# Scaling the gradient before its transposes, and placing filler steps by a PE budget, in a fused attention and FFN backward kernel

## The chip, the cores and the metric

The kernel runs on one core of a Trainium2 chip. The metric is the device time of one execution in microseconds (us). Every time below is the median of several runs, and a span is the length of the one profiled run. The granted TensorE clock and the span are listed for each run. A run that is more than 1.5% above the fastest of its kernel counts as slow and is left out of ratios.

The engines go by the names of the profile: PE (TensorE) does the matmuls, DVE (VectorE) and POOL (GpSimd) element-wise work, ACT (ScalarE) exponentials and copies, and SP (SyncE) issues DMAs, as ACT and POOL also do here. SBUF is the working memory on the chip; PE writes its results to PSUM, in banks. An "extra" is a DVE operation other than the product Pd that runs between two products. A "ring" is a circle of steps in which each waits for the one before.

## The reference

The forward function mixes windowed attention and a gated FFN with a sigmoid gate. The kernel returns the output and the gradients of seven inputs, so eight tensors.

```python
# S = 2048, D = 512, H = 32 heads of 16, window 256, F = 1376, bf16
g = sigmoid((x * gate_w).sum(-1, keepdims=True))
qkv = x @ wqkv                                  # A: attention
p = softmax(where(band_of_256, q @ k.T * 16**-0.5, -1e9))
a = (p @ v) @ wo
gate, up = x @ W_gate, x @ W_up                 # B: FFN
b = (gate * (gate > 0) * up) @ W_down
out = g * a + (1 - g) * b
out, vjp = jax.vjp(forward, x, wqkv, wo, W_gate, W_up, W_down, gate_w)
return out, *vjp(grad_out)
```

## The kernel before

The kernel has four stages. A **start** transposes `x` and `grad_out` and computes the first of four projections. An **attention loop** of 384 slots follows. A slot computes scores S and score gradients dP for one unit, the exponential Pt of S on ACT, a mask on POOL and the product Pd of Pt and dP on DVE. Sums over Pt and Pd feed small per-stage tasks. FFN and further projection work fills PE between them. A **transition** loads and transposes weights and the attention results. Then come the **dw pass** (weight gradients) and the **output pass** (output and dx).

```python
# one slot: PE writes S and dP, ACT makes Pt, POOL masks it, DVE makes Pd
u.S  = ps.tile([P, 2, W], F32, tag="S",  bufs=1)       # two PSUM banks
u.dP = ps.tile([P, 2, W], F32, tag="dP", bufs=1)       # two PSUM banks, one buffer
nc.scalar.activation(u.Pt[:, :, :u.width], u.S[:, :, :u.width], ACT.Exp)
nc.gpsimd.affine_select(...)                            # mask, in place on Pt
nc.vector.tensor_tensor(out=u.Pd[...], in0=u.Pt[...], in1=u.dP[...], op=ALU.mult)

# the FFN step that the change makes lighter on DVE
dhs = fp.tile([P, W], BF, tag="dhs", bufs=1)
nc.vector.scalar_tensor_tensor(out=dhs[:fs, :], in0=g_bc[:fs, sl], scalar=1.0, in1=dhps[:fs, :],
                               op0=ALU.subtract, op1=ALU.mult, reverse0=True)

# what fills PE in each slot: one projection step if one is open, then FFN by even share
def fill(frac):
    if projs:
        try: next(projs[0])
        except StopIteration: projs.pop(0)
    while dense["done"] < frac * TOTAL:
        dense["done"] += next(ffn)        # front of a chunk in turn with the back of the one before
# ... (cut)

# transition: SP loads dqT, dkvT, OT; ACT's queue loads the weights
for c in range(DC):
    nc.sync.dma_start(dqT[:, c, :], dqo_v[0, c])
# ... dkvT, OT (cut)
nc.scalar.dma_start(Wg_sb6[:], ...)
nc.scalar.dma_start(Wu_sb6[:], ...)
nc.scalar.dma_start(wqkv_sb6[:], ...)
nc.scalar.dma_start(Wd_sb[:, :nfull, :], ...)
nc.scalar.dma_start(Wd_sb[:fsz(nfull), nfull, :], ...)   # the last part of Wd
nc.scalar.dma_start(wo_sb6[:], ...)
# then PE transposes Wg, Wu, wqkv; ACT and DVE copy the results in turn
```

Of the kernel before, what the change touches and what calls it, by code (L numbers as in the profile page):

```python
# [46 lines left out]
def kernel(  # L47
# [64 lines left out]
    with ExitStack() as win:  # L112
# [23 lines left out]
        big = win.enter_context(tc.tile_pool(name="big", bufs=1))  # L136
        x_T = big.tile([P, DC, S], BF, name="x_T")
        go_T = big.tile([P, DC, S], BF, name="go_T")
        db_r = big.tile([P, NT, D], BF, name="db_r")
        g_bc = big.tile([P, S], F32, name="g_bc")  # L140

        ps = win.enter_context(tc.tile_pool(name="ps", bufs=1, space=PSUM))
        wp = win.enter_context(tc.tile_pool(name="wp", bufs=2))
        fp = win.enter_context(tc.tile_pool(name="fp", bufs=2))
        ap_ = win.enter_context(tc.tile_pool(name="ap", bufs=2))
# [45 lines left out]

        flip = {"i": 0}
# [8 lines left out]
        def rows_to_T(dst, src, sb):  # L201
            for cp in range(2):
                pt = tr_bank(8)
                for c in range(2):
                    for k in range(4):
                        nc.tensor.transpose(pt[:, 4 * c + k, :], src[:, 4 * sb + k, (2 * cp + c) * P:(2 * cp + c + 1) * P],
                                            ident[:])
                evac2(dst[:, 2 * cp:2 * cp + 2, sb * W:(sb + 1) * W].rearrange("p c s -> p c s"),
                      pt.rearrange("p (c k) s -> p c (k s)", c=2))

        def proj(c, evac):
            w3, wo_r = wsets.pop(("p", c))
            pt = tr_bank(4)
            for jc in range(DC):
                nc.tensor.transpose(pt[:, jc, :], wo_r[:, jc * P:(jc + 1) * P], ident[:])
            woT = wp.tile([P, DC, P], BF, tag="woT")
            evac(woT[:], pt)
            yield 0.3
            for sb in range(NSB):
                sl = slice(sb * W, (sb + 1) * W)  # L220
                for which in (1, 2, 0, 3):
                    pp = mm_bank()
                    for cd in range(DC):
                        if which < 3:
                            nc.tensor.matmul(pp[:], lhsT=w3[:, cd, which, :], rhs=x_T[:, cd, sl],  # L225
                                             start=(cd == 0), stop=(cd == DC - 1))
                        else:
                            nc.tensor.matmul(pp[:], lhsT=woT[:, cd, :], rhs=go_T[:, cd, sl],
                                             start=(cd == 0), stop=(cd == DC - 1))
                    cs = wp.tile([P, W], BF, tag="cs", bufs=2)  # L230
                    if which == 0:
                        nc.scalar.mul(cs[:], pp[:], scale)
                    elif which < 3:
                        evac(cs[:], pp[:])
                    else:
                        nc.vector.tensor_tensor(out=cs[:], in0=pp[:], in1=g_bc[:, sl], op=ALU.mult)  # L236
                    dst_d, w = ((QD_d, 0), (KV_d, 0), (KV_d, 1), (QD_d, 1))[which]
                    nc.sync.dma_start(dst_d[c][sb].rearrange("(h w d) s -> w h d s", w=2, d=Dh)[w], cs[:])
                    yield 0.87

        def ffn_front(fc):
            fs, f0 = fsz(fc), fc * P
            wg, wu, wd = wsets.pop(("f", fc))
            if fc + 1 < FC:
                load_ffn(fc + 1)
            pt = tr_bank(4)
            for c in range(DC):
                nc.tensor.transpose(pt[:, c, :fs], wd[:fs, c * P:(c + 1) * P], ident[:fs, :fs])
            wdT = wp.tile([P, DC, P], BF, tag="wdT")
            nc.scalar.copy(wdT[:, :, :fs], pt[:, :, :fs])  # L250
            yield 0.3
            rows = []
            for tg in range(NSB):
                sl = slice(tg * W, (tg + 1) * W)
                hT = fp.tile([P, W], BF, tag="hT")
                dgT = fp.tile([P, W], BF, tag="dgT")
                duT = fp.tile([P, W], BF, tag="duT")
                gps = mm_bank()
                for c in range(DC):
                    nc.tensor.matmul(gps[:fs, :], lhsT=wg[:, c, :fs], rhs=x_T[:, c, sl],  # L260
                                     start=(c == 0), stop=(c == DC - 1))
                rg = fp.tile([P, W], BF, tag="rg")
                nc.scalar.activation(rg[:fs, :], gps[:fs, :], ACT.Relu)
                yield 0.87
                ups = mm_bank()
                for c in range(DC):
                    nc.tensor.matmul(ups[:fs, :], lhsT=wu[:, c, :fs], rhs=x_T[:, c, sl],
                                     start=(c == 0), stop=(c == DC - 1))
                upm = fp.tile([P, W], BF, tag="upm")
                nc.vector.scalar_tensor_tensor(out=upm[:fs, :], in0=rg[:fs, :], scalar=0.0,  # L270
                                               in1=ups[:fs, :], op0=ALU.is_gt, op1=ALU.mult)
                nc.gpsimd.tensor_tensor(out=hT[:fs, :], in0=rg[:fs, :], in1=upm[:fs, :], op=ALU.mult)  # L272
                yield 0.87
                dhps = mm_bank()
                for c in range(DC):
                    nc.tensor.matmul(dhps[:fs, :], lhsT=wdT[:, c, :fs], rhs=go_T[:, c, sl],
                                     start=(c == 0), stop=(c == DC - 1))
                dhs = fp.tile([P, W], BF, tag="dhs", bufs=1)
                nc.vector.scalar_tensor_tensor(out=dhs[:fs, :], in0=g_bc[:fs, sl], scalar=1.0, in1=dhps[:fs, :],  # L279
                                               op0=ALU.subtract, op1=ALU.mult, reverse0=True)  # L280
                nc.vector.tensor_tensor(out=dgT[:fs, :], in0=dhs[:fs, :], in1=upm[:fs, :], op=ALU.mult)
                nc.gpsimd.tensor_tensor(out=duT[:fs, :], in0=dhs[:fs, :], in1=rg[:fs, :], op=ALU.mult)  # L282
                for w, src_t in enumerate((hT, dgT, duT)):
                    nc.sync.dma_start(ffn_d[fc, w, :fs, sl], src_t[:fs, :])
                rw = fp.tile([P, 4, 3, P], BF, tag="rows", bufs=6)
                if fs == P:
                    nc.sync.dma_start_transpose(out=rw[:].rearrange("p k w f -> p k (w f)"),
                                                in_=ffn_d[fc, :, :, sl].rearrange("w p s -> (w p) s"))
                else:
                    for w in range(3):  # L290
                        nc.sync.dma_start_transpose(out=rw[:, :, w, :fs], in_=ffn_d[fc, w, :fs, sl])
                rows.append(rw)
                yield 0.87
            wsets["r", fc] = rows

        def ffn_back(fc):
            fs, f0 = fsz(fc), fc * P
            rows = wsets.pop(("r", fc))
            wst = fp.tile([P, DC, 2, P], BF, tag="wst", bufs=1)
            for c in range(DC):  # L300
                wps = mm_bank()
                for t in range(NT):
                    nc.tensor.matmul(wps[:, 0:2 * fs], lhsT=x_r[:, t, c * P:(c + 1) * P],  # L303
                                     rhs=rows[t // 4][:, t % 4, 1:3, :fs], start=(t == 0), stop=(t == NT - 1))
                    if t == NT // 2 - 1:
                        yield 0.9
                nc.scalar.copy(wst[:, c, :, :fs], wps[:, 0:2 * fs].rearrange("p (a f) -> p a f", a=2))
                yield 0.9
            nc.sync.dma_start(out_4[:, f0:f0 + fs].rearrange("(c p) f -> p c f", p=P), wst[:, :, 0, :fs])
            nc.sync.dma_start(out_5[:, f0:f0 + fs].rearrange("(c p) f -> p c f", p=P), wst[:, :, 1, :fs])  # L310
            dps = mm_bank()
            for t in range(NT):
                nc.tensor.matmul(dps[:fs, :D], lhsT=rows[t // 4][:, t % 4, 0, :fs], rhs=db_r[:, t, :],  # L313
                                 start=(t == 0), stop=(t == NT - 1))
                if t % 4 == 3 and t < NT - 1:
                    yield 0.87
            dst = fp.tile([P, D], BF, tag="dst", bufs=1)
            nc.scalar.copy(dst[:fs, :], dps[:fs, :D])
            nc.sync.dma_start(out_6[f0:f0 + fs, :], dst[:fs, :])
            yield 0.87  # L320
# [520 lines left out]
```

## Time and profile before

| | before |
|---|---|
| median of the first 4 runs | 1201.27 us (1195.23 to 1206.71) |
| profiled span | 1193.5 us |
| first Pd starts | 51.1 us |
| last Pd ends | 840.3 us |
| first dw matmul | 908.8 us |
| first matmul of the output pass | 1003.4 us |

These moments are read from the instruction timeline. The stages therefore last 51, 789, 68.5, 95 and 190 us.

First, four lines of the profile page of the kernel before. Line one is the span. The second gives busy time, share of the span and number of instructions per engine. The other two cut the span into 40 slices of 30 us: busy tenths of PE, and the granted PE clock in tenths.

```profile
span 1193.5 us, 25074 instructions
...
PE 1002.2 (84%) x9607; PEld 469.9 (39%) x9748; DVE 707.7 (59%) x876; ACT 562.6 (47%) x751; POOL 633.8 (53%) x1019
...
PE   5688789999888888888889999889128886999997
...
PEclk9889999999999999999999999999657999999999
...
```

PE is busy nearly all the time except in the slices after the loop, where its clock falls too. That is the transition.

The table of stretches of the kernel before gives, for each stretch, its length, then busy time and (in brackets) instruction count per engine, then the granted clock, the DMA share and GB/s.

```profile
...
core 0: us, PE busy (x) PEld busy (x) DVE busy (x) ACT busy (x) POOL busy (x), PEclk, DMA share, GB/s
100.00:700.00 600.00, 531.65 (x6214) 242.83 (x6308) 476.65 (x516) 383.23 (x490) 438.83 (x725) 0.99 0.49 123
845.00:905.00 60.00, 15.43 (x120) 12.80 (x121) 7.17 (x18) 8.70 (x15) 7.80 (x11) 0.50 0.79 257
...
```

In 600 us of the loop PE is busy 89% and DVE 79%. In the transition PE has half its clock and is busy 26%. The Trainium skill, page "TensorE: Matmul & The Clock Gate", section "What's actually happening", says that PE falls to half rate after an idle window of about 3.4 us. The trace agrees on the half rate: the clock is 0.50 here and 0.99 in the loop. How long an idle stretch it takes is not read from this table.

The longest of PE's waits in the loop of the kernel before, 130 to 775 us (who waits for whom, total us, number, longest):

```profile
...
PE dP L424 <- DVE Pd L462: 32.4, 87, 1.0
...
```

Two lines of the groups of the same loop, shapes kept apart: busy us and mean ns of one, then idle time of the engine just before them and what ended it.

```profile
...
L462 DVE TENSOR_TENSOR Pd<-Pt,dP 128x1024 bf16<-128x1024 bf16 x242 | 294.7, 1218 | 84.4 <-PE dP L424 39.8 <-PE S L424 23.6 <-ACT Pt L457 7.1
...
L279 DVE SCALAR_TENSOR_TENSOR dhs<-g_bc,mm 128x512 bf16<-128x512 f32 x33 | 22.5, 683 | 1.9 <-PE mm L276 1.5
...
```

The product takes 1.22 us, and the step to be removed from DVE takes 0.68.

The instruction timeline of the transition of the kernel before (start, duration, engine and line, operation; in brackets the idle time before and what ended it; ACTq and SPq are DMA issues):

```profile
...
847.86 0.46 ACTq L668 DMA_DIRECT2D Wg_sb<-in_B_W_gate_dram  x1
848.37 0.52 ACTq L669 DMA_DIRECT2D Wu_sb<-in_B_W_up_dram  x1
...
868.90 0.38 ACTq L670 DMA_DIRECT2D wqkv_sb<-in_A_wqkv_dram  x1
...
876.80 0.37 ACTq L671 DMA_DIRECT2D Wd_sb<-in_B_W_down_dram  x1
877.21 8.34 ACTq L673 DMA_DIRECT2D Wd_sb<-in_B_W_down_dram  x1
887.01 0.49 ACTq L674 DMA_DIRECT2D wo_sb<-in_A_wo_dram  x1
...
887.55 1.07 ACT L650 COPY WgT_sb<-pt 128x512 bf16<-128x512 bf16 x2 [45.75 <-DMA Wd_sb<-in_B_W_down_dram]
888.18 2.12 PE L679 MATMUL pt<-ident,Wg_sb 128*128 128x128 bf16 x14 [16.95 <-ACT WgT_sb L650]
...
```

ACT's DMA issues run from 847.86 to 887.01, and ACT's first copy waits behind them. PE could go on with the weight transposes only at 888.18.

### The profile page before, as it was taken

The numbers are of one execution on the slowest core, as the hardware profiler recorded it, in microseconds if no ns is written. First come the engines' busy times: TensorE is split into PE (matmuls) and PEld (weight loads), VectorE is DVE, ScalarE is ACT, GpSimd is POOL, SyncE is SP. The second block draws the span as 40 slices with busy tenths as digits, with TensorE's granted clock in tenths as the row PEclk, the third lists the DMA queues.
The fourth block names the chain that finished last, engine by engine and source line by source line (L and its number), as shares of the span: only waits on it lengthen the run. The fifth ranks groups of instructions, "written<-read, shape, count | busy, mean of one in ns | idle before, by whom it ended". The sixth has DMA issues, their size and how long they took to land. (4 is left out here: it accounts for less than half of the span.)

```text
span 1193.5 us, 25074 instructions
## 1 busy us (share of the span) xinstructions
PE 1002.2 (84%) x9607; PEld 469.9 (39%) x9748; DVE 707.7 (59%) x876; ACT 562.6 (47%) x751; POOL 633.8 (53%) x1019
## 2 busy tenths in 40 slices
PE   5688789999888888888889999889128886999997
PEld 4233434434343443433444343444025442444443
DVE  2247787867788866788788888787102122222322
ACT  5345667666666655666666666665013221111010
POOL 2736787856777855778777778675110001221221
PEclk9889999999999999999999999999657999999999
DMA  7257554454643544445553544322780014545330
GB/s 203 77 136 187 124 128 122 112 143 109 132 120 104 134 124 119 121 107 123 122 129 103 127 103 123 85 74 63 197 308 34 19 45 135 175 130 159 102 107 23
DMA packets 267242, 142.81 MB, mean 120 GB/s; under 512 B 161201, under 2 KB 261970, under 8 KB 267122
## 3 DMA queue, kind: packets, MB, share of 16 engines
q1 hardware_dynamic: 236514, 115.08, 37.2%
q10 hardware_dynamic: 28224, 19.70, 5.4%
q0 software_dynamic: 2384, 6.43, 1.7%
q8 instruction: 76, 1.25, 0.5%
q14 instruction: 44, 0.36, 0.1%
HBM read 59.05 MB, written 52.59 MB: 94 GB/s over the span
## 5 line engine op out<-in xcount | busy, mean ns | idle before, releaser
L462 DVE TENSOR_TENSOR Pd<-Pt,dP 128x1024 bf16<-128x1024 bf16 (+2 forms) x384 | 442.0, 1151 | 145.2 <-PE dP L424 76.0
L457 ACT ACTIVATE Pt<-S 128x1024 bf16<-128x1024 f32 (+2 forms) x384 | 372.6, 970 | 203.1 <-PE S L424 174.0
L434 POOL TENSOR_SCALAR_AFFINE_SELECT Pt<-Pt 128x256 bf16<-128x256 bf16 (+1 forms) x736 | 348.3, 497 | 165.3 <-ACT Pt L457 158.0
L303 PE MATMUL mm<-rw,x_r 128*128 128x256 bf16 (+1 forms) x704 | 101.7, 272 | 5.9 <-DMA rw<-ffn_d 5.8
L424 PEld LDWEIGHTS <-kv 32*128 32x128 bf16 x1408 | 54.3, 92 | 116.9 <-issue 109.3
L424 PE MATMUL dP<-dO,kv 32*128 32x128 bf16 (+2 forms) x704 | 74.5, 275 | 25.8 <-DVE Pd L462 22.4
L424 PE MATMUL dP<-kv,dO 32*128 32x384 bf16 (+2 forms) x704 | 73.0, 273 | 17.0 <-DVE Pd L462 14.5
L771 ACT COPY a_sb<-aps 128x512 f32<-128x512 f32 x16 | 9.4, 586 | 160.9 <-issue 78.6
L424 PE MATMUL S<-Q,kv 32*128 32x128 bf16 (+2 forms) x704 | 79.3, 276 | 4.6 <-ACT Pt L457 3.5
L424 PE MATMUL S<-kv,Q 32*128 32x384 bf16 (+2 forms) x704 | 76.9, 275 | 2.6 <-ACT Pt L457 1.9
L303 PEld LDWEIGHTS <-x_r 128*128 128x128 bf16 x704 | 59.3, 98 | 40.9 <-issue 28.5
L705 POOL DMA_DIRECT2D go_t<-in_grad_out_dram x16 | 8.7, 543 | 121.1 <-DVE da_t L707 105.9
L797 PE MATMUL dxps<-WgT_sb,dgT_g 128*128 128x512 bf16 (+1 forms) x176 | 66.7, 379 | 0.8
L272 POOL TENSOR_TENSOR hT<-rg,upm 128x512 bf16<-128x512 bf16 (+1 forms) x44 | 50.8, 1155 | 21.6 <-DVE upm L270 21.2
L797 PE MATMUL dxps<-WuT_sb,duT_g 128*128 128x512 bf16 (+1 forms) x161 | 61.0, 379 | 0.0
L282 POOL TENSOR_TENSOR duT<-dhs,rg 128x512 bf16<-128x512 bf16 (+1 forms) x44 | 52.2, 1185 | 11.2 <-DVE dhs L279 10.6
L777 POOL DMA_DIRECT2D out_dram<-o_sb x16 | 8.7, 542 | 90.4 <-DVE o_sb L775 62.5
L713 PE MATMUL dw<-rt,x_r 128*128 128x512 bf16 x184 | 46.0, 387 | 12.3 <-ACT rt L650 11.8
L225 PE MATMUL mm<-x_T,w 128*128 128x512 bf16 x183 | 49.9, 389 | 7.3 <-DVE cs L236 1.8
L775 DVE SCALAR_TENSOR_TENSOR o_sb<-bps,omg_all,ga 128x512 bf16<-128x512 f32 x16 | 12.0, 751 | 73.7 <-ACT ga L773 72.0
L424 PEld LDWEIGHTS <-dO 32*128 32x128 bf16 x704 | 29.7, 91 | 65.6 <-issue 62.4
L313 PE MATMUL mm<-db_r,rw 128*128 128x512 bf16 (+1 forms) x163 | 48.8, 383 | 1.6 <-issue 1.6
(147 smaller groups left out, 1557.2 us busy)
## 6 DMA issues: line engine op xcount, KB each, us to landing
ffn_d<-hT SPq DMA_DIRECT2D x40, 128.0 KB
ffn_d<-dgT SPq DMA_DIRECT2D x40, 128.0 KB
ffn_d<-duT SPq DMA_DIRECT2D x40, 128.0 KB
hT_g<-ffn_d SPq DMA_DIRECT2D x8, 640.0 KB
dgT_g<-ffn_d ACTq DMA_DIRECT2D x8, 640.0 KB
duT_g<-ffn_d ACTq DMA_DIRECT2D x8, 640.0 KB
KV_d<-cs SPq DMA_DIRECT2D x32, 128.0 KB
QD_d<-cs SPq DMA_DIRECT2D x32, 128.0 KB
```

Source lines behind the costliest of these rows:

```text
L225: nc.tensor.matmul(pp[:], lhsT=w3[:, cd, which, :], rhs=x_T[:, cd, sl], start=(cd == 0), stop=(cd == DC - 1))
L272: nc.gpsimd.tensor_tensor(out=hT[:fs, :], in0=rg[:fs, :], in1=upm[:fs, :], op=ALU.mult)
L282: nc.gpsimd.tensor_tensor(out=duT[:fs, :], in0=dhs[:fs, :], in1=rg[:fs, :], op=ALU.mult)
L303: nc.tensor.matmul(wps[:, 0:2 * fs], lhsT=x_r[:, t, c * P:(c + 1) * P], rhs=rows[t // 4][:, t % 4, 1:3, :fs], start=(t == 0), stop=(t == N ...
L313: nc.tensor.matmul(dps[:fs, :D], lhsT=rows[t // 4][:, t % 4, 0, :fs], rhs=db_r[:, t, :], start=(t == 0), stop=(t == NT - 1))
L424: lst.append(lambda lt=lt, ls=ls, rt=rt, rsl=rsl, i=i, rs=rs, col=col, cnt=cnt: nc.tensor.matmul(bank[:, i % 2, col * P:(col + cnt) * P], ...
L434: nc.gpsimd.affine_select(out=v.rearrange("p h (b k) -> p h b k", b=cnt), in_=v.rearrange("p h (b k) -> p h b k", b=cnt), compare_op=ALU.i ...
L457: nc.scalar.activation(u.Pt[:, :, :u.width], u.S[:, :, :u.width], ACT.Exp)
L462: nc.vector.tensor_tensor(out=u.Pd[:, :, :u.width], in0=u.Pt[:, :, :u.width], in1=u.dP[:, :, :u.width], op=ALU.mult)
L713: nc.tensor.matmul(banks[c][:], lhsT=x_r[:, t, c * P:(c + 1) * P], rhs=rt[:].rearrange("p a b -> p (a b)"), start=(t == 0), stop=(t == NT ...
L775: nc.vector.scalar_tensor_tensor(out=o_sb[:], in0=bps[:], scalar=omg_all[:, t:t + 1], in1=ga[:], op0=ALU.mult, op1=ALU.add)
L797: nc.tensor.matmul(dxps[:], lhsT=l_, rhs=r_, start=(i == 0), stop=(i == len(pairs) - 1))
```

## The change: its intent, and the diff

The change has four parts.

1. `grad_out` is scaled by (1-g) once, before it is transposed, so the FFN step `dhs` no longer needs the gate and becomes a copy on ACT.
2. Projection, FFN and attention tasks become step objects that state their PE time and their DVE, ACT and POOL operations. A fill rule places them by a running PE budget, and prefers a step that leaves at most one extra operation per engine in a slot. Attention tasks are split into more steps. S of the next unit and dP of the present one are still traced in turn, as before, but they alternate in more slots.
3. At the start, projection 0 is woven with the transposes, and some work moves from POOL to DVE.
4. The SBUF pools are reordered, so that the buffers for the weights of the transition are free earlier. Two ordering hints (`issue_after`) at the start of the transition are new as well.

```diff
-                dhs = fp.tile([P, W], BF, tag="dhs", bufs=1)
-                nc.vector.scalar_tensor_tensor(out=dhs[:fs, :], in0=g_bc[:fs, sl], scalar=1.0, in1=dhps[:fs, :],
-                                               op0=ALU.subtract, op1=ALU.mult, reverse0=True)
+                dhs = fp.tile([P, W], BF, tag="dhs", bufs=1, name="dhs")
+                nc.scalar.copy(dhs[:fs, :], dhps[:fs, :])
 ... (cut: the same steps as objects)
-        def fill(frac):
-            if projs:
-                try:
-                    next(projs[0])
-                except StopIteration:
-                    projs.pop(0)
-            while dense["done"] < frac * TOTAL:
-                try:
-                    dense["done"] += next(ffn)
-                except StopIteration:
-                    dense["done"] = 1e9
+        def fill(slot, used):
+            todo["due"] += todo["all"] / nslots
+            while todo["all"] - todo["pe"] + 0.44 < todo["due"]:
+                cands = candidates(slot)
+                if not cands:
+                    break
+                fit = [q for q in cands if used["dve"] + q[0].dve <= 1 and used["act"] + q[0].act <= 1
+                       and used["pool"] + q[0].pool <= 1]
+                q = (fit or sorted(cands, key=lambda q: q[0].dve + q[0].act))[0]
+                s_ = q.pop(0)
+                run(s_, used)
+                if q is front and len(front) % nfront == 0:
+                    ready_at[FC - 1 - len(front) // nfront] = slot + 4
+            todo["slot"] -= 1
 ... (cut: start)
+        ps = win.enter_context(tc.tile_pool(name="ps", bufs=1, space=PSUM))
+        ap_ = win.enter_context(tc.tile_pool(name="ap", bufs=2))
+        ph1 = win.enter_context(ExitStack())
+        big = ph1.enter_context(tc.tile_pool(name="big", bufs=1))
 ... (cut)
+        wp = ph1.enter_context(tc.tile_pool(name="wp", bufs=2))
+        fp = ph1.enter_context(tc.tile_pool(name="fp", bufs=2))
 ... (cut: tasks t0 to t7; the transition's loads themselves are not changed)
```

The budget counts projections too: `todo["all"]` includes them, so a slot with a projection step gets less FFN.

## The prediction

> **What bounds it now.** The instruction timeline splits the 1193.5 us profile into start (first product Pd at 51.1), attention loop of 384 slots (last Pd ends 840.3), transition (PE nearly idle until the first dw matmul, 908.8), dw and output passes. In the loop PE is 87 to 92% busy (table of stretches), but DVE sets the pace: dP has one PSUM buffer, so product (1.22 us), release, dP matmuls and next product make a ring. Start to start, 130 to 815 us: a 1024-wide Pd with no other DVE work behind it takes 1.80 us (median; 0.58 waiting for PE), with one other operation 1.86, with two 2.45, with three 3.3. One extra operation hides in the PE gap; a second costs 0.6 us. Groups of 32 slots take 56 to 62 us, but the first 100.5, and 64 to 70 where projection steps come on top of an even share of FFN.
>
> **What the change does.**
> 1. grad_out is scaled by (1-g) before its transpose, so dhs becomes an ACT copy: 44 DVE operations of 0.68 us leave, 44 ACT copies of about 0.59 come. Sigmoid passes on 512 columns: 12 become 4.
> 2. Attention tasks, projection and FFN become steps placed by PE budget, at most one extra DVE/ACT/POOL operation per slot. In the built order, gaps between Pd with two or more extras fall from 63 to 37 (extras 276 to 228). Score blocks whose S and dP alternate over the four row groups rise from about 70 to 190. The Trainium skill, TensorEngine Tiling (Array Packing), Overview, says tiles operate independently in parallel; the trace agrees: an alternating block of eight lets PE go on after 0.34 us; dP and S apart cost 0.32 each. That is about 30 us of PE time, partly hidden under DVE.
> 3. Start: projection 0 is woven with the x transposes; db_r scaling moves from POOL (16 x 1.56 us) to DVE. The first dP still waits for DMAs that SP issues one by one (0.45 us each), so first Pd stays near 50 us; later slots run faster.
> 4. Pools are reordered. Before, ACT's weight-load issues stood behind a 6.5 us DMA wait, then Wu waited for a dqT load, wqkv for Wg's landing, Wd for Wu's, wo for wqkv's; ACT's copies stood behind those, so transposes resumed only at 888. After, Wg, Wu and wqkv issue nearly back to back after the last FFN store.
>
> **Costing.** Loop: mean gap by class (0 extras: 1.79, 1: 1.94, 2: 2.50, 3: 3.3) times new counts (196, 150, 33, 4) is about 735 us against 761 for the old; start excess falls from about 40 to 20. Loop end about 793: -47. Transition: first dw about 40 us after the loop instead of 68: -28. Later passes unchanged. All of it is critical. 1193.5 - 75 = 1118.
>
> **Prediction: 1118 us, 80% range 1080 to 1160.** Faster by over 2%: 0.93; within: 0.05; slower: 0.02.
>
> **Right if:** last Pd ends near 795; groups of 32 slots take 57 to 62 us, the first under 85; weight transposes run steadily from about 17 us after the loop; DVE busy about 684 us, ACT about 583; output pass still about 190.
>
> **Wrong if:** alternating blocks make PE wait for the later of exp and product (slots 1.95+); ACT, at one extra per slot, becomes the ring; SP issue holds the start; or 14 MB of loads, not issue order, limit the transition (first dw still 60+ us after the loop): then 1140 to 1160.

## The result, and the profile after

The new kernel takes 1148.19 us (median of 10 runs, 1144.88 to 1151.37; two more fast ones, 1147.20 and 1155.23) against 1199.30 for the one before (16 runs). The ratio is 0.9565, with a 95% interval of 0.954 to 0.959. A ratio is the mean time of one kernel's fast runs over that of the other's of the same rounds, so it is not quite the ratio of the medians. The time lies in the predicted range, 30 us above its middle.

| moment or stage, us | before | after | difference | predicted |
|---|---|---|---|---|
| first Pd starts | 51.1 | 51.0 | -0.1 | near 50 |
| last Pd ends | 840.3 | 800.3 | -40.0 | 793 (-47) |
| transition, to the first dw | 68.5 | 57.9 | -10.6 | 40 (-28) |
| dw pass | 94.6 | 93.6 | -1.0 | unchanged |
| output pass to the end | 190.1 | 191.4 | +1.3 | unchanged, about 190 |
| end of span | 1193.5 | 1143.2 | -50.3 | 1118 |

The page of the new kernel, the same four lines:

```profile
span 1143.2 us, 25111 instructions
...
PE 964.7 (84%) x9640; PEld 464.0 (41%) x9748; DVE 682.9 (60%) x844; ACT 579.9 (51%) x791; POOL 608.1 (53%) x1003
...
PE   5888899888988888899888888888058886999997
...
PEclk9999999999999999999999999998559998999999
...
```

DVE fell to 682.9 us and ACT rose to 579.9, as costed (684 and 583). The low slices at three quarters of the span are still there.

The table of stretches of the new kernel, columns as before:

```profile
...
100.00:700.00 600.00, 528.59 (x6423) 250.89 (x6491) 471.44 (x495) 409.95 (x543) 452.36 (x748) 0.99 0.51 126
...
805.00:855.00 50.00, 16.00 (x126) 13.38 (x127) 7.45 (x18) 8.69 (x15) 5.64 (x7) 0.50 0.94 248
...
```

In the same 600 us PE is as busy as before, 88%. The Trainium skill, page "Perfetto Trace Analysis", section "Identifying the Most-Contended Engine", warns that matmul busy share does not tell how near PE is to its limit. The share stays at 88 to 89%, while the loop is 40 us shorter.

The same wait in the loop of the new kernel, and the groups of the product and of the `dhs` copy:

```profile
...
PE dP L444 <- DVE Pd L484: 43.4, 114, 1.4
...
```

```profile
...
L484 DVE TENSOR_TENSOR Pd<-Pt,dP 128x1024 bf16<-128x1024 bf16 x246 | 299.6, 1218 | 91.7 <-PE dP L444 35.5 <-PE S L444 32.1 <-POOL Pt L456 7.0
...
L275 ACT CAST dhs<-mm 128x512 bf16<-128x512 f32 x34 | 19.9, 584 | 5.8 <-PE mm L253 3.9 <-issue 1.1 <-PE dP L444 0.4
...
```

PE waits longer for the product than before (43.4 us, not 32.4), and the product has its old length. So the slot did not get faster of itself. Where the loop's 40 us came from is shown by the time that each group of 32 slots takes, start to start of Pd, from the timeline's records:

| 32 slots, us | 1st | 2nd | 3rd | 4th | 5th | 6th | 7th | 8th | 9th | 10th | 11th | 12th |
|---|---|---|---|---|---|---|---|---|---|---|---|---|
| before | 96.8 | 59.4 | 68.6 | 64.1 | 59.0 | 69.2 | 67.7 | 59.6 | 61.4 | 60.4 | 60.9 | 61.2 |
| after | 68.5 | 60.7 | 63.8 | 59.5 | 61.4 | 64.8 | 61.4 | 62.1 | 62.6 | 60.7 | 58.7 | 64.2 |

(The last group ends at the start of its last product. The prediction's 100.5 us for the first group is not what these records give.) The first group gains 28.3 us. The four groups that also carry projections 2 and 3 (3rd, 4th, 6th and 7th) gain 20.1. The seven others lose 8.5. In the first group of the kernel before, one single slot takes 16.1 us (from 68.1): between two products PE works through projection and FFN steps there. The longest slot of the new kernel takes 6.0 us.

The transition of the new kernel, the same view as of before:

```profile
...
799.65 0.42 ACTq L734 DMA_DIRECT2D Wg_sb<-in_B_W_gate_dram  x1
...
800.70 0.37 ACTq L735 DMA_DIRECT2D Wu_sb<-in_B_W_up_dram  x1
801.11 1.13 ACTq L736 DMA_DIRECT2D wqkv_sb<-in_A_wqkv_dram  x1
...
807.21 1.01 PE L745 MATMUL pt<-ident,Wg_sb 128*128 128x128 bf16 x8 [6.56 <-DMA Wg_sb<-in_B_W_gate_dram]
...
808.71 2.54 SPq L720 DMA_DIRECT2D dqT<-DQO_d  x4
...
811.35 0.41 ACTq L737 DMA_DIRECT2D Wd_sb<-in_B_W_down_dram  x1
...
829.44 0.34 ACTq L739 DMA_DIRECT2D Wd_sb<-in_B_W_down_dram  x1
836.52 0.39 ACTq L740 DMA_DIRECT2D wo_sb<-in_A_wo_dram  x1
836.94 1.07 ACT L714 COPY WgT_sb<-pt 128x512 bf16<-128x512 bf16 x2 [35.66 <-DMA Wd_sb<-in_B_W_down_dram]
837.58 2.78 PE L745 MATMUL pt<-ident,Wg_sb 128*128 128x128 bf16 x20 [27.68 <-ACT WgT_sb L714]
...
```

Wg, Wu and wqkv are now issued within two microseconds, and PE starts to transpose at 807.21, only 7 us after the loop. But then ACT stands at the last issues of its queue until 836.52, and PE resumes at 837.58. In the built program each DMA of these queues raises one of eight completion semaphores, and an issue waits until the earlier DMA on its semaphore has landed. The last part of Wd shares one with the second dqT load, and wo with the third. No data ties them.

### The profile page after: what moved, and what is told of

Same layout as the page of the kernel before. It is cut to its first block, busy times and chain, and to the rows that moved or that the text cites. A ratio compares the mean times of both kernels' runs of the same rounds, so it can differ in the third digit from the quotient of the medians.

```text
span 1143.2 us, 25111 instructions
## 1 busy us (share of the span) xinstructions
PE 964.7 (84%) x9640; PEld 464.0 (41%) x9748; DVE 682.9 (60%) x844; ACT 579.9 (51%) x791; POOL 608.1 (53%) x1003
## 5 line engine op out<-in xcount | busy, mean ns | idle before, releaser
L484 DVE TENSOR_TENSOR Pd<-Pt,dP 128x1024 bf16<-128x1024 bf16 (+2 forms) x384 | 441.9, 1151 | 148.0 <-PE dP L444 68.4
L309 PE MATMUL mm<-rows,x_r 128*128 128x256 bf16 (+1 forms) x704 | 97.0, 276 | 5.3 <-DMA rows<-ffn_d 5.3
L444 PEld LDWEIGHTS <-kv 32*128 32x128 bf16 x1408 | 52.0, 91 | 114.6 <-issue 104.1
L444 PE MATMUL S<-kv,Q 32*128 32x384 bf16 (+2 forms) x704 | 83.1, 278 | 9.7 <-ACT Pt L479 8.8
L444 PE MATMUL S<-Q,kv 32*128 32x128 bf16 (+2 forms) x704 | 82.1, 275 | 5.9 <-ACT Pt L479 5.1
L309 PEld LDWEIGHTS <-x_r 128*128 128x128 bf16 x704 | 63.0, 99 | 34.4 <-issue 21.5
L444 PEld LDWEIGHTS <-dO 32*128 32x128 bf16 x704 | 34.1, 92 | 78.8 <-issue 74.9
L714 ACT COPY rt<-pt 128x512 bf16<-128x512 bf16 x32 | 18.8, 588 | 64.6 <-PE pt L745 64.6
```

What stands on the lines that cost most here:

```text
L309: nc.tensor.matmul(v["b"][:, 0:2 * fs], lhsT=x_r[:, t, c * P:(c + 1) * P], rhs=rows[t // 4][:, t % 4, 1:3, :fs], start=(t == 0), stop=(t = ...
L444: lst.append(lambda lt=lt, ls=ls, rt=rt, rsl=rsl, i=i, rs=rs, col=col, cnt=cnt: nc.tensor.matmul(bank[:, i % 2, col * P:(col + cnt) * P], ...
L484: last["dve"] = nc.vector.tensor_tensor(out=u.Pd[:, :, :u.width], in0=u.Pt[:, :, :u.width], in1=u.dP[:, :, :u.width], op=ALU.mult)
L714: nc.scalar.copy(out, in_)
```

## The experiments

Each was sent beside runs of the kernel before on the same chip. "Loop end" is the end of the last Pd in the profiled run. One caution on single profiles: three kernels with the loop order of the new kernel ended the loop at 800.3, 801.1 and 803.1, but two with the order of before ended it at 840.3 and 848.1.

### tail_sp: the last weight loads on the other queue

```diff
         for c in range(DC):
             nc.sync.dma_start(OT[:, c, :], dqo_v[1, c])
+        nc.sync.dma_start(Wd_sb[:, :nfull, :], ...)
+        nc.sync.dma_start(Wd_sb[:fsz(nfull), nfull, :], ...)
+        nc.sync.dma_start(wo_sb6[:], ...)
...
-            nc.scalar.dma_start(Wd_sb[:, :nfull, :], ...)
-            nc.scalar.dma_start(Wd_sb[:fsz(nfull), nfull, :], ...)
-            nc.scalar.dma_start(wo_sb6[:], ...)
```

> The changed kernel, with only the loads of Wd and wo moved from ACT's queue to the end of SP's loads, so that ACT's copies of the weight transposes no longer stand behind their issue. The instruction order of the attention loop is the same. Theory A (issue order on ACT holds the transition): transposes run from about 10 us after the last Pd, the first dw comes 36 to 42 us after the loop's end instead of 58, total about 1128 us (ratio to the changed kernel 0.98). Rival B (the volume of loads holds it): the first dw stays within 5 us of 58, total 1143 or more.

Measured: correct, 1137.87 us, ratio 0.9511 [0.9471, 0.9551]. The loop ends at 801.1 and the first dw comes at 840.5, so the transition lasts 39.4 us, not 57.9. The timeline of its transition:

```profile
...
807.92 1.01 PE L745 MATMUL pt<-ident,Wg_sb 128*128 128x128 bf16 x8 [6.47 <-DMA Wg_sb<-in_B_W_gate_dram]
...
809.47 0.58 ACT L714 COPY WgT_sb<-pt 128x512 bf16<-128x512 bf16 x1 [7.39 <-DMA DKV_d<-dkv]
...
810.09 1.01 PE L745 MATMUL pt<-ident,Wg_sb 128*128 128x128 bf16 x8 [1.16 <-DVE WgT_sb L716]
...
811.35 1.01 PE L745 MATMUL pt<-ident,Wg_sb 128*128 128x128 bf16 x8 [0.25 <-ACT WgT_sb L714]
...
839.54 0.72 PE L745 MATMUL pt<-ident,dqT 128*128 128x128 bf16 x5 [3.58 <-DMA dqT<-DQO_d]
...
```

ACT's first copy comes at 809.47 instead of 836.94, and PE's transposes go on every 1.26 us. Now the last of the four dqT loads is what ends the transition: the transposes at 839.54 waited 3.58 us for it. The whole span is 15.6 us shorter. So the edit takes 18.5 us off the new kernel's transition. One caution: the moved loads are now issued at 845.60 and later, so the edit also takes their traffic out of the transition. By SP's next issue on the same semaphore, the last dqT load had landed 41.7 us after the loop in the new kernel (841.97) and 38.4 after it here (839.51). So an estimate is that about 15 of the 18.5 us were ACT standing at DMA issues, and about 3 the lighter traffic. The profiled run was the fastest of the four; by the medians the gain on the new kernel is 10 us, and by the two ratios 6.5 (0.54% of 1199). The other runs have no trace, so where they lose the rest is not known.

### before_tail_sp: the same edit on the kernel before

> The kernel before, with only the loads of Wd and wo moved from ACT's queue to the end of SP's. Theory A (ACT's copies behind the issue of loads): wqkv still waits for Wg's landing at 29 us after the loop, then copies are free, so the first dw comes about 50 to 55 us after the loop instead of 68, total minus 12 to 20 us against before. Rival B (the volume of loads): minus 5 us or less.

The edit is the same. Measured: correct, 1189.07 us, ratio 0.9882 [0.9846, 0.9919]. Its transition lasts 56.6 us instead of 68.5 (848.1 to 904.7). The edit is therefore worth 12 us of the transition in the kernel before, and 18.5 in the new one.

### pools_old: the old order of the pools

```diff
         ps = win.enter_context(tc.tile_pool(name="ps", bufs=1, space=PSUM))
-        ap_ = win.enter_context(tc.tile_pool(name="ap", bufs=2))
         ph1 = win.enter_context(ExitStack())
         big = ph1.enter_context(tc.tile_pool(name="big", bufs=1))
...
         fp = ph1.enter_context(tc.tile_pool(name="fp", bufs=2))
+        ap_ = win.enter_context(tc.tile_pool(name="ap", bufs=2))
```

> The changed kernel, with the attention pool opened after the projection and FFN pools again, as before. The built order of DVE, ACT and PE in the loop is the same; only addresses differ, and with them the waits in front of the loads of the last part. Theory A (the pool order is what shortened the transition): loop within 3 us, last Pd to first dw goes from 58 back to about 68 us, total plus 8 to 12 us. Rival B (it came from elsewhere): within 3 us.

Measured: correct, 1159.63 us, ratio 0.9651 [0.9611, 0.9691]. The loop ends at 803.1, and the transition lasts 67.2 us, again nearly the 68.5 of before. Wg is issued at 815.98 instead of 799.65. So the pools are nearly the whole gain of the change in the transition, 9 of 10.6 us, and none of the loop's.

### dhs_dve: the lighter step back on DVE

```diff
-                nc.scalar.copy(dhs[:fs, :], dhps[:fs, :])
+                nc.vector.tensor_copy(dhs[:fs, :], dhps[:fs, :])
```

> The changed kernel, with dhs copied by DVE instead of ACT; steps and budgets unchanged. In the built order gaps between Pd with two or more extra DVE operations rise from 37 to 65. Theory A (DVE's ring with dP sets the pace, two extras cost 0.6 us): loop longer by 15 to 22 us, total about 1167 us. Rival B (PE sets the steady pace, the DVE operations that left were hidden): within 5 us of 1148.

Measured: correct, 1155.38 us, ratio 0.9645 [0.9614, 0.9677]; the loop ends at 812.5, 12 us later. The direction is that of theory A and the size is below it. By the same count as in the prediction, the gaps with two or more extras rise from 37 to 65. The edit adds 44 x 0.68 = 30 us of DVE work (the duration is that of the step in the kernel before), of which the loop pays 12.

### start_apart: projection 0 not woven with the transposes

```diff
             rows_to_T(x_T, x_r, sb)
-            for k in range(3):
-                p0[1 + 4 * sb + k].fn()
...
             rows_to_T(db_T, db_r, sb)
-            p0[4 + 4 * sb].fn()
+        for s_ in p0[1:]:
+            s_.fn()
```

> The changed kernel, with projection 0 no longer woven with the x transposes but after both transposes. Theory A (the weaving gives the faster start): the first 32 products, 68.5 us now, go towards 85 to 97 or the first Pd comes 5 to 10 us later, total plus 12 to 28 us. Rival B (the start is faster because steps are spread by budget, SP's DMA issues hold the first product in any case): total plus 6 us at most.

Measured: correct, 1155.71 us, ratio 0.9647 [0.9619, 0.9675]. The first Pd comes earlier (38.9 us), but its first two groups take 79.4 and 69.3 us, so slot 64 is reached at 187.6 instead of 180.2. By the end of the loop (811.2) it is 10.9 us behind, and by the ratios 10. So the weave is worth 7 to 11 us, a little less than theory A expected. The kernel before reached slot 64 at 207.3, so most of the 27 us there has another cause.

### apart: S and dP traced one after the other

```diff
-                weave((second(cur[4]) if cur else []) + (first(nxt[4]) if nxt else []))
+                if cur:
+                    weave(second(cur[4]))
+                if nxt:
+                    weave(first(nxt[4]))
```

> The changed kernel, with the S block of matmuls traced after the dP block instead of alternating with it: alternating blocks fall from 209 to 48 of the built order. Theory A (alternating saves PE time that counts): about 160 blocks times 0.2 to 0.3 us, a third to all of it visible, total plus 12 to 40 us. Rival B (the saved PE time is hidden under DVE's ring, or paid back by waiting for the later of exp and product): within 5 us, or faster.

Measured: correct, 1143.39 us, ratio 0.9497 [0.9447, 0.9547]; the loop ends at 797.8. The edit takes alternating blocks from 209 to 48 by count of the built program, and nothing is lost. But the trace shows that it did not take the overlap away. By start times of the matmuls, S and dP mix (in more than two runs) in 261 of 453 blocks here, against 223 of 501 in the new kernel: where S is traced right after dP, its first matmul often starts about 16 ns after the first of dP, and PE goes on after about 0.34 us all the same. (The record does not show whether the compiler or PE brings this about.) PE's time on S and dP between 130 and 700 us, in the new kernel and then here (length, PE busy, PEld busy, clock, DMA share, GB/s), and its wait for the product here:

```profile
...
130.00:700.00 570.00, 172.10 (x2168) 68.13 (x2168) 0.99 0.50 125
...
```

```profile
...
130.00:700.00 570.00, 152.63 (x2176) 64.89 (x2176) 0.99 0.52 125
...
```

```profile
...
PE dP L444 <- DVE Pd L484: 61.7, 159, 1.1
...
```

So this run saves 19 us of PE time on the score blocks, PE waits 25 us longer for the product (36.5 in the new kernel), and the loop ends only 2.5 us earlier. PE time saved inside these blocks came back as waiting. What alternation is worth against blocks that do not overlap at all, the prediction's 30 us, was not tested.

### no_ring: a product that does not read dP (wrong)

```diff
-  in0=u.Pt[:, :, :u.width], in1=u.dP[:, :, :u.width],
+  in0=u.Pt[:, :, :u.width], in1=u.Pt[:, :, :u.width],
```

> The changed kernel, wrong on purpose: the product multiplies Pt by itself in place of Pt by dP, so that DVE does not wait for the dP matmuls nor they for DVE. All matmuls and all other work stay. Theory A (the ring of one dP buffer between DVE and PE sets the steady pace of about 1.9 us a slot): slots fall to the next limit, 1.65 to 1.75 us, loop about 60 us shorter, total near 1085. Rival B (PE's own stream sets the pace): slots stay at 1.85 or more, total 1130 or more.

Measured: wrong, 1177.89 us, ratio 0.98 [0.9766, 0.9834]. It is slower than the new kernel, so it answers another question. Groups of the loop with shapes kept apart, the new kernel first and then this one:

```profile
...
L456 POOL TENSOR_SCALAR_AFFINE_SELECT Pt<-Pt 128x256 bf16<-128x256 bf16 x392 | 164.4, 432 | 77.5 <-ACT Pt L479 77.1 <-DVE upm L268 0.2
...
```

```profile
...
L484 DVE TENSOR_TENSOR Pd<-Pt 128x1024 bf16<-128x1024 bf16 x238 | 248.3, 1043 | 146.0 <-POOL Pt L456 139.8 <-ACT Pt L479 4.9 <-ACT ri L515 0.5
...
L456 POOL TENSOR_SCALAR_AFFINE_SELECT Pt<-Pt 128x256 bf16<-128x256 bf16 x380 | 215.7, 582 | 21.1 <-ACT Pt L479 20.9
...
```

The product did get shorter (1043 ns), but the same mask on POOL took 582 ns instead of 432, and DVE then waited 139.8 us for it. The Trainium skill, page "SBUF — State Buffer", section "Who interferes with whom", says that a DVE instruction with two SBUF inputs contends with a GpSimd instruction that reads SBUF, and that one with at most one SBUF input, outside the 2-port modes, does not. The numbers fit: the edit turned the PSUM input into a second SBUF input. The granted clock in its loop was lower too, 0.93 against 0.99. The run is therefore inconclusive on the ring.

### half_pd: half a product, still read from PSUM (wrong)

```diff
-  out=u.Pd[:, :, :u.width], in0=u.Pt[:, :, :u.width], in1=u.dP[:, :, :u.width],
+  out=u.Pd[:, 0, :u.width], in0=u.Pt[:, 0, :u.width], in1=u.dP[:, 0, :u.width],
...
-  m = u.Pd if use_pd else u.Pt
+  m = u.Pd if use_pd and i % 2 == 0 else u.Pt
```

> Wrong result on purpose (dQ, dK and dV side of half the heads). The product Pd covers one of the two 512-column halves, and the sums over the other half read Pt. DVE still reads dP from PSUM, so no new collision on SBUF as in the earlier run that read Pt twice. The product takes about 0.66 instead of 1.15 us; everything else of a slot stays. Theory A (the ring product, release, dP matmuls sets the pace): the gap without extras falls from 1.80 to about 1.3 until PE (88% busy) stops it, mean wide gap 1.97 to about 1.75, loop end near 730, time 1070 to 1090. Rival B (the order of PE work sets the pace and DVE only follows): gap without extras 1.65 or more, loop end above 775, time above 1122.

Measured: wrong, 1106.79 us, ratio 0.9216 [0.9179, 0.9253]; the loop ends at 754.2. The product's line on the profile page:

```profile
...
L484 DVE TENSOR_TENSOR Pd<-Pt,dP 128x512 bf16<-128x512 bf16 (+2 forms) x384 | 250.2, 652 | 245.0 <-PE S L444 104.7
...
```

All products together fall from 441.9 us (the new kernel's page) to 250.2, that is by 192, and the loop falls by 46. A quarter of what DVE saves reaches the loop. The median gap without extras is 1.50 us. The new kernel's is 1.80 for wide products alone, and this kernel's mixes in narrow ones. So neither theory holds: the loop gains 46 us, where A expected about 70 (an end near 730) and B at most 25. The profile puts the longest idle time of DVE down to a score matmul S, but the product reads no S. In 77 of the 108 waits put down to S between 130 and 700 us, a dP matmul ended within 150 ns of the product's start too, so most of them can be waits for dP, whose block S shares. The product ring is a limit, but not the pace by itself.

### split_pd: two products on two single banks

```diff
-  u.dP = ps.tile([P, 2, W], F32, tag="dP", bufs=1, name="dP")
+  u.dP = [ps.tile([P, W], F32, tag=f"dP{h}", bufs=1, name=f"dP{h}") for h in range(2)]
...
+  for h in range(2):
+      nc.vector.tensor_tensor(out=u.Pd[:, h, :u.width], in0=u.Pt[:, h, :u.width], in1=u.dP[h][:, :u.width], op=ALU.mult)
```

> Correct result. dP is two tiles of one PSUM bank each instead of one of two banks, and the product is two operations of 512 columns. DVE work per slot rises from 1.15 to about 1.38 us, but PE may refill the first bank while DVE reads the second. Theory A (ring): the wait of DVE for dP shrinks from 0.6 to 0.2 us or less, slots without extras about 1.5, with one extra about 2.1; with 228 extras over 384 slots the mean is about 1.8, loop end 740 to 775, time 1090 to 1125. Rival B (PE order sets the pace): same as the new kernel within 10 us, or slower by up to 20 for the added DVE time.

Measured: correct, 1151.04 us, ratio 0.9576 [0.9539, 0.9613]; the loop ends at 796.6. The waits of DVE in its loop, then those of the new kernel in the same stretch:

```profile
...
DVE Pd L485 <- PE S L444: 42.0, 58, 2.8
DVE Pd L485 <- PE dP L444: 20.5, 38, 1.8
...
```

```profile
...
DVE Pd L484 <- PE dP L444: 43.4, 69, 1.3
DVE Pd L484 <- PE S L444: 34.7, 53, 2.3
...
```

The wait for dP halved, from 43.4 to 20.5 us, while that put down to S grew from 34.7 to 42.0. As in half_pd, most waits put down to S can be waits for dP (43 of 58 here, 37 of 53 in the new kernel), so the two are better read together: 78.1 us before the edit, 62.5 after. The time did not move, as rival B said. But the edit does two things: it opens the ring, and it raises DVE's time on products from 441.9 to 468.2 us. The median gap without extras falls from 1.80 to 1.68 us, and that with one extra rises from 1.80 to 1.86. At the price found in dhs_dve (40%) the 26 us would cost about 10, so an estimate of what the ring alone is worth is of that size. The run does not separate the two.

### fill_old: the old fill rule, first try

The edit calls, in place of the budget rule, one projection step per slot when one is open, then FFN steps by even share, taking front and back steps in turn.

> The changed kernel, with the old filling rule: one projection step forced in each slot while there are any, and FFN steps by an even share of all slots, front and back in turn. Theory A (levelling is what shortened the projection stretches and part of the start): the groups of 32 slots with projection (first, 3rd, 4th, 6th, 7th) go up by 3 to 8 us each, the others down by 1 to 2, total plus 12 to 25 us. Rival B (total PE work is the same, the loop is bound by the sum): within 5 us.

Measured: correct, 1219.78 us, ratio 1.0174 [1.0132, 1.0216]. It is slower than the kernel before, so it does not undo the change; it adds something of its own:

```profile
...
PE mm L309 <- DMA rows<-ffn_d: 31.6, 9, 5.4
...
```

The same wait is 2.0 us in the new kernel in the same stretch, 130 to 775 us. The try drew back steps of a chunk directly after its last front step, before the rows had come through DRAM. Seven slots of the stretch took 5.2 to 8.4 us, and one before it 13.6. It shows what the margin of four slots in the new rule protects from, and not what the rule gains.

### fill_zip: the old fill rule in the old order

```diff
+        ffn_seq = list(front[:nfront])
+        for fc in range(1, FC):
+            # ... the front of fc in turn with the back of fc - 1
+        def fill_zip(slot, used):
+            if projs:
+                projs.pop(0).fn()
+            while dense["done"] < slot / len(seq) * 229.0 and ffn_seq:
+                s_ = ffn_seq.pop(0)
+                s_.fn()
+                dense["done"] += s_.pe
...
-                fill(g + 1, used)
+                fill_zip(g + 1, used)
```

> Repair of the earlier run with the old fill rule, whose FFN order was not that of the kernel before: its weight-gradient matmuls started right after the last store of the same chunk and PE waited 31.6 us for the transposed rows (2.0 in the new kernel), which hid the effect of placement. Here the steps of the new kernel run in exactly the old order (front of a chunk in turn with the back of the chunk before), an even share per slot and one projection step forced in each slot after a projection is opened. Gaps with two or more extra DVE operations: 41 (37 in the new kernel). Theory A (the slot budget is what shortened the first slots and the projection groups): first 32 slots 80 to 88 us, projection groups 4 to 6 us longer each, other groups unchanged, loop end 820 to 835 us, time 1165 to 1185. Rival B (the gain came from the lighter FFN step and the new start alone): loop end within 6 us of 800, time 1145 to 1156.

Measured: correct, 1187.21 us (1178.28 to 1197.47; one of the four runs counted as slow), ratio 0.9841 [0.9778, 0.9904]. The loop ends at 831.8, 31.5 us later than in the new kernel and 8.5 earlier than before. Its groups of 32 slots:

| 32 slots, us | 1st | 3rd, 4th, 6th, 7th together | the other seven |
|---|---|---|---|
| before | 96.8 | 269.6 | 421.9 |
| fill_zip | 84.4 | 267.6 | 428.2 |
| after | 68.5 | 249.5 | 430.4 |

The new rule gains 16 us on it in the first group (projection 1 lies there) and 18 in the groups with projections 2 and 3, and nothing elsewhere. These are close to theory A's numbers, but the repair was not complete. PE's wait for the transposed rows over the whole loop, from first to last Pd, in the kernel before, in this one and in the new one:

```profile
...
PE mm L303 <- DMA rw<-ffn_d: 5.8, 3, 2.8
...
```

```profile
...
PE mm L309 <- DMA rows<-ffn_d: 24.9, 8, 9.1
...
```

```profile
...
PE mm L309 <- DMA rows<-ffn_d: 5.3, 3, 3.3
...
```

The longest of them, 9.1 us, makes one slot of the first group 11.8 us long. This wait is of the edit's own making: the kernel before, with the old order, has as little of it as the new one. It is 19.6 us longer than in the new kernel, where the loops differ by 31.5, so an estimate of what the placement itself is worth in the whole loop is 12 us. In the projection groups, where the wait is only 2.6 us, about 15 of the 18 us are left; in the first group about 7 of 16. The granted clock also differs, 0.96 in this loop and 0.99 in the new one; but the 3rd, 4th and 6th groups ran at full clock in both, and 13 of the 18 us lie there. The transition of this kernel is long again (69.2 us), because here wqkv shares a semaphore with Wg and was issued only at 844.48, when Wg had landed. Which loads share one depends on how many DMAs came before, so an edit of the loop can shift it.

### final: what paid, together

The three edits are those of tail_sp and apart, and this one:

```diff
-  nc.sync.dma_start(do0[...], QD_d[...])
+  (nc.gpsimd if n < 3 else nc.sync).dma_start(do0[...], QD_d[...])
```

> Correct result. Three edits on the new kernel: the Wd and wo loads at the end of SP's loads (worth 18.5 us of the transition alone), S and dP traced apart (loop end 797.8 instead of 800.3 alone), and the dO loads of the first three stages issued by POOL's queue instead of SP's. First: transition 38 to 41 us, as when the loads were moved alone; the two earlier gains add up: end near 1123, median of runs 1118 to 1130. The third edit: Theory A (SP's serial issues hold the first slots, as the prediction said): first Pd at 42 to 47 us instead of 50 to 51 and the 64th slot done 3 us or more before 180, loop end 789 to 795. Rival B (PE's queue of start work holds the first slots; when first Pd came at 38.9 us with the projection apart, the 64th slot was not earlier): first Pd may be earlier, the 64th slot within 3 us of 180 to 183, loop end 796 to 801.

Measured: correct, 1128.99 us (6 runs), ratio 0.9412 [0.9371, 0.9453], the fastest correct kernel. The loop ends at 797.4 and the transition lasts 40.5 us, as expected. The third edit did nothing, as rival B said: first Pd at 51.5, slot 64 at 178.3. POOL's queue shows what held the load:

```profile
...
47.65 1.96 POOL L401 DMA_DIRECT2D dO<-QD_d  x4 [5.16 <-DMA QD_d<-cs]
...
```

POOL had been idle for 5.16 us, waiting for the projection's store to land, and issued dO at 47.65; SP had issued it at 48.02 in the new kernel. So it was the store that the load reads after, and not SP's order of issues. Also, the dw pass took 99.6 us here instead of 93.6. The chain that ended last shows the first store of gradients in flight for 6.41 us there, while the moved weight loads ran. wo had been issued at 858.47 and that store at 861.13. So part of the gain of tail_sp is given back there, it seems to this traffic, which was not tested; in tail_sp's own run it was 1.7 us (dw pass 95.3).

## Why the prediction was right or wrong

**The time.** The prediction of 1118 was 25 us too fast against the profiled 1143.2. The terms of its sum: loop end 793 predicted and 800.3 measured (+7.3); transition 40 and 57.9 (+17.9); later passes 284.7 and 285.0 (+0.3).

**The step that failed: "Transition: first dw about 40 us after the loop instead of 68: -28."** It measured -10.6. The first half of its reasoning held: "After, Wg, Wu and wqkv issue nearly back to back", at 799.65, 800.70 and 801.11, and pools_old shows that the pools did it. But the reasoning stopped at the first three issues. The same queue holds three more, two of them had to wait until dqT loads landed at 829 and 836, and ACT's copies stand behind them, so "weight transposes run steadily from about 17 us after the loop" was 37 us. tail_sp shows it: with those issues moved, the transition is 39.4 us, and the volume of loads, which the prediction named as the other danger, accounts for about 3 us by the estimate above. The time landed in the 1140 to 1160 us of "Wrong if", but for the issue order and not for the volume named there. The prediction had described this very mechanism for the kernel before, and did not carry it to the end of the new queue.

**The loop: right size, wrong reason in part.** Predicted -47, measured -40; that the size came so near is partly luck, as the costing behind it does not hold. "DVE sets the pace: dP has one PSUM buffer, so product, release, dP matmuls and next product make a ring" is too strong. 192 us less of products shortened the loop by 46, and DVE work put back cost 40% of itself: DVE counts, but not at its full price. Split banks gained nothing on the whole, though with 26 us more of DVE time. On the other side, PE time saved on score blocks (apart) came back as waiting for the product, which speaks for the ring as a part of the pace. The count of extras between products also fails as a cost model. With the prediction's class means (1.79, 1.94, 2.50, 3.3 us) the counts of fill_zip (197, 145, 40, 1) and of the new kernel (196, 150, 33, 4) both give 737 us, but their loops differ by 31.5, of which 19.6 us are fill_zip's own wait for rows. In the groups with projections, what did the work is that PE's filler is levelled: a projection step no longer comes on top of a full FFN share. The profile before had shown it, in the groups of 64 to 70 us, and the prediction named it, but priced it through DVE. Of the 27 us by which slot 64 comes earlier than before, the weave accounts for about 7, and the placement for about 4 (an estimate: slot 64 is 12.6 us later in fill_zip, 9.1 of them its wait for rows). No run isolates the rest, and its cause stays open.

**The start: right, and larger.** "Start excess falls from about 40 to 20" was a gain of 20 where the first group gained 28. First Pd stayed at 51, as said. The cause given, that SP issues the dO loads one by one, was wrong: the load waited for a store to land.

**Alternating score blocks** were counted nearly right (about 190 forecast, 209 by the later count). The prediction left open how much would hide, and used the Trainium skill, "TensorEngine Tiling (Array Packing)", for it. That tiles work in parallel stands there in "Key Properties"; the "Overview" that the prediction names only calls them independent. Blocks do overlap as that page says, in apart too (0.34 us for eight matmuls, 0.32 for four alone), but time of a block is not time of the loop.

**Busy times** (DVE 684, ACT 583) came within 4 us, the output pass was 191.4 as said, and groups of 57 to 62 us were 58.7 to 64.8 after the first.

## What to carry to other kernels

When an engine both issues DMAs and does work that others wait for, follow its queue to the last issue, and ask of each what it must wait for, the completion semaphores of unrelated transfers included; moving three issues to another queue shortened a stage by 18 us here. When PE and DVE hand tiles to each other in a loop, a shorter operation on one of them returned a quarter of its saving here, while levelling PE's filler across the slots took about 15 us out of the groups that had carried too much of it. Test a suspected ring with an edit that keeps the memories it reads the same, or the edit makes a new collision. And look in the trace of every undoing run for waits of its own before its whole loss is put down to what it undid: here they were 19.6 of 31.5 us.

## What the Trainium skill lacked or had wrong

- "DMA: Bandwidth & Descriptors", section "Issuing engines are not separate DMA queues", says that starting DMAs from several engines saves only the sequencer time to start them, usually small beside the transfer. Moving the dO loads to POOL indeed gained nothing (first Pd at 51.0 and 51.5 us). It lacks that a DMA issue which waits holds up its engine's other work: moving three issues off ACT shortened the transition from 57.9 to 39.4 us.
- No page that was read says that the builder shares eight completion semaphores among the DMAs of these queues, so that an issue can wait for an unrelated transfer. The runs show it at 829.44 and 836.52 us in the new kernel, and at 844.48 in fill_zip.
- "SBUF — State Buffer", section "Who interferes with whom", fits what no_ring shows of two-input DVE operations and GpSimd. The sizes it gives (6.8 times slower for DVE, 1.5 for GpSimd) are single measurements without their operations. Here, in a stream of both, the mask rose from 432 to 582 ns, 1.35 times.
